# First image by image rows, first tile in float32, and MLP weights rebuilt from integer words: a pooled-attention + MLP kernel

## Chip, core and metric

The kernel runs on one core of a Trainium2 chip. The metric is the device time of one launch in microseconds (us), the median of several runs; lower is better. The engines are named as in the profile: PE (TensorE; PEld is its weight load), DVE (VectorE), ACT (ScalarE), POOL (GpSimd) and SP (SyncE, which issues the DMAs). Each engine works through its own instructions in order and waits where an operand or a buffer is not ready.

## What is computed

```python
# q (4, 12288, 128), kv (4, 384, 32, 128), w_sr (128, 128): float32
kv_pool = kv.reshape(B, H // 4, 4, W // 4, 4, C).mean(axis=(2, 4))
k = v = kv_pool.reshape(B, -1, C) @ w_sr             # 768 keys per image
s = (q @ k.transpose(0, 2, 1)) / np.sqrt(C)
a = np.exp(s - s.max(-1, keepdims=True))
a /= a.sum(-1, keepdims=True) + 1e-09
x = (a @ v).reshape(49152, 128)
h = x @ w_in                                         # w_in (128, 2048): float64
g = 0.5 * h * (1.0 + erf(h / np.sqrt(2.0)))
out = g @ w_out                                      # w_out (2048, 128): float64
```

The two weight matrices arrive as float64. [...]

## The kernel before

The 49152 tokens go in 96 tiles of 512 (24 tiles per image). A tile passes: queries scaled and split into a float16 high and low part, turned by a DMA transpose (`q_max`, `q_scale`, `q_split`, `q_turn`); scores of 128 tokens at a time against the 768 keys, as three float16 products (`score`, L365); evacuation with the running minimum (`evac`, L378); `exp`; division and split into float16 parts (`attn_hi`, `attn_lo`); a DMA transpose (`attn_turn`); the product with the values (`av`, 18 matmuls of 512 columns); `x_out`; then for each of 16 blocks of the MLP `mlp_in` (three matmuls), `gelu`, a float16 split (`rest`) and `mlp_out` (three matmuls).

All instructions stand in an order written by hand. The table `START` (L22) holds the order up to the first block of tile 1; behind it a loop (L737) runs tiles 1 to 95, in which each `mlp_in` of a tile stands beside the `mlp_out` six blocks back (`LAG`), beside the scores of the tile two ahead and the `av` of the next one. "Loop start" below is the first `mlp_in` of tile 1, the first row behind `START` on PE.

In `START` the first image is loaded in 24 DMAs of 256 KB (`kv_load_first`, L174), in which a partition receives 2 KB runs (four pixels of one row). DVE adds the 16 pixels of a pool window (`kv_sum_part`, L184), PE turns the sum, ACT scales it, PE multiplies by `w_sr` (`kv_key`) into `kT`, the keys in float32. Only when the largest key of the image is known (`kv_max`, `kv_bound`) can the keys be split in float16 (`kv_high`, `kv_low`) and the scores of tile 0 begin.

The weights are built in eight pieces of 512 columns (`w_split`, L649): ACT makes the absolute value of the upper word and a scaled lower word; DVE shifts and masks the words to a float32; ACT or DVE scales and casts to the float16 high part; POOL makes the low part with three float32 operations (L681 to L683). `w_max` and `w_scale` find the scale first. All eight pieces stand inside `START`, between the blocks of tile 0.

PSUM: `ps_h` has three buffers for blocks and half scores, `ps_s` one for the scores of 128 tokens, so the next `score` waits for the `evac` of the last.

Of the kernel before, what the change touches and what calls it, by code (L numbers as in the profile page):

```python
# [9 lines left out]
F32 = mybir.dt.float32  # L10
# [12 lines left out]
    ("q_load", 0), ("kv_load", 0), ("kv_load", 1), ("w_sr",), ("kv_load", 2),  # L23
    ("q_max", 0), ("q_scale", 0), ("q_split", 0), ("kv_load", 3), ("kv_load", 4), ("kv_load", 5),
    ("q_load", 1), ("kv_load", 6), ("q_turn", 0), ("kv_load", 7), ("kv_load", 8), ("kv_load", 9),
    ("kv_load", 10), ("kv_load", 11), ("wi_load", 0), ("wi_load", 1), ("wi_load", 2),
    ("wi_load", 3), ("q_load", 2), ("wo_load", 0), ("wo_load", 1),
    ("kv_sum", 0, 0), ("kv_sum", 0, 1), ("kv_sum", 1, 0), ("kv_turn", 0), ("kv_key", 0),
    ("kv_sum", 1, 1), ("kv_sum", 2, 0), ("kv_sum", 2, 1), ("kv_turn", 1), ("kv_key", 1),
    ("q_max", 1), ("q_scale", 1), ("q_split", 1), ("kv_turn", 2), ("kv_sum", 3, 0),  # L30
    ("kv_sum", 3, 1), ("kv_key", 2), ("kv_max", 0), ("kv_sum", 4, 0), ("kv_turn", 3),
    ("kv_key", 3), ("kv_sum", 4, 1), ("q_turn", 1), ("kv_sum", 5, 0), ("kv_sum", 5, 1),
    ("kv_turn", 4), ("kv_key", 4), ("kv_turn", 5), ("kv_key", 5), ("kv_max", 1), ("kv_bound", 0),
    ("w_split", 0, 0), ("kv_bound", 1), ("w_max", 0), ("kv_bound", 2), ("kv_high", 0),
# [791 lines left out]
```

## Time and profile before

| | |
|---|---|
| runs (us) | 2857.69, 2857.76, 2859.03; median 2857.76 |
| span of the profiled execution | 2856.5 us, first to last instruction |
| the profiled execution's own time | not listed apart from the runs; the median stands 1.26 us over its span |
| busy: PE, DVE, ACT, POOL | 2771.2, 2427.1, 2527.1, 891.6 us |
| in the stretch 165 to 2800 us | PE 2633.29 of 2635.00 us busy |

A row of the timeline gives the start, the time taken, engine, line, operation, what is written and read, and in brackets how long the engine sat idle before it and what released it. A row of the windows gives a stretch, then the busy time and number of instructions of each engine, the granted clock of PE, the DMA share and GB/s. A row of the groups gives busy time and mean duration.

### The profile page before, as it was taken

The numbers are of one execution on the slowest core, as the hardware profiler recorded it, in microseconds if no ns is written. First come the engines' busy times: TensorE is split into PE (matmuls) and PEld (weight loads), VectorE is DVE, ScalarE is ACT, GpSimd is POOL, SyncE is SP. The second block draws the span as 40 slices with busy tenths as digits, with TensorE's granted clock in tenths as the row PEclk, the third lists the DMA queues.
The fourth block names the chain that finished last, engine by engine and source line by source line (L and its number), as shares of the span: only waits on it lengthen the run. The fifth ranks groups of instructions, "written<-read, shape, count | busy, mean of one in ns | idle before, by whom it ended". The sixth has DMA issues, their size and how long they took to land.

```text
span 2856.5 us, 37679 instructions
## 1 busy us (share of the span) xinstructions
PE 2771.2 (97%) x13390; PEld 1316.0 (46%) x13390; DVE 2427.1 (85%) x3565; ACT 2527.1 (88%) x3414; POOL 891.6 (31%) x825
## 2 busy tenths in 40 slices
PE   3699999999999999999999999999999999999999
PEld 2244444444444444444444444444444444444444
DVE  7988888898888888889888888888888888888885
ACT  2589999999999999999999999999999999999997
POOL 2544343222233434222223343413222222222221
PEclk9799999999999999999999999999999999999999
DMA  7165555445445555445445655544544444444442
GB/s 198 35 124 109 105 108 107 91 94 98 93 106 109 105 124 106 95 91 100 91 95 102 124 105 107 106 95 87 104 92 94 92 94 93 94 92 94 90 93 49
DMA packets 854717, 284.90 MB, mean 100 GB/s; under 512 B 814848, under 2 KB 817280, under 8 KB 854528
## 3 DMA queue, kind: packets, MB, share of 16 engines
q1 hardware_dynamic: 854528, 282.49, 48.6%
q8 instruction: 105, 1.72, 0.2%
q14 instruction: 84, 0.69, 0.1%
HBM read 54.59 MB, written 25.17 MB: 28 GB/s over the span
## 4 chain that ended last, share of the span: by engine, by line
PE 91%; DVE 4%; DMA 2%; ACT 1%; issue 1%; POOL 1%; SPq 0%; DVEq 0%; POOLq 0%; ACTq 0%
PE s L372 12%; PE px L492 12%; PE po L542 11%; PE po L543 11%; PE po L544 11%; PE h L513 11%; PE h L512 11%; PE h L511 11%; DMA kv<-in_kv_dram 1%; DVE gl L531 1%; DVE a L454 1%; DMA q_v<-q_u 0%; DVE a L450 0%; DMA q<-in_q_dram 0%; DVE sn L383 0%
## 5 line engine op out<-in xcount | busy, mean ns | idle before, releaser
L525 ACT ACTIVATE g<-h,hs 128x512 f32<-128x512 f32 x1536 | 1007.1, 681 | 236.7 <-PE h L513 198.5
L531 DVE SCALAR_TENSOR_TENSOR gl<-g,gs,gh 128x1024 f16<-128x1024 f32 x768 | 1017.1, 1337 | 27.0 <-ACT gh L527 18.5
L527 ACT ACTIVATE gh<-g,gs 128x1024 f16<-128x1024 f32 x768 | 881.9, 1148 | 25.2
L544 PE MATMUL po<-gh,wo_l 128*128 128x512 f16 x1536 | 583.4, 380 | 13.6 <-POOL wo_l L683 13.6
L542 PE MATMUL po<-gh,wo_h 128*128 128x512 f16 x1536 | 582.9, 380 | 4.7 <-DVE wo_h L678 2.9
L511 PE MATMUL h<-xh,wi_h 128*128 128x512 f16 x1536 | 583.9, 380 | 1.2 <-DVE sn L419 0.6
L512 PE MATMUL h<-xl,wi_h 128*128 128x512 f16 x1536 | 583.5, 380 | 0.4 <-DVE xl L503 0.4
L513 PE MATMUL h<-xh,wi_l 128*128 128x512 f16 x1536 | 583.2, 380 | 0.0
L543 PE MATMUL po<-gl,wo_h 128*128 128x512 f16 x1536 | 582.8, 379 | 0.2 <-DVE gl L531 0.2
L345 POOL TENSOR_TENSOR q<-q,qi 128x512 f32<-128x512 f32 x96 | 100.9, 1051 | 1481.6 <-DVE qi L337 1288.8
L383 DVE TENSOR_SCALAR_CACHE_REDUCE sn<-s,sg 128x768 f32<-128x768 f32 x378 | 382.7, 1013 | 71.1 <-PE s L372 67.8
L372 PE MATMUL s<-k,q_v 128*128 128x384 f16 x2268 | 434.3, 328 | 6.5 <-DVE sn L383 5.1
L454 DVE SCALAR_TENSOR_TENSOR a<-sn,r,a 128x768 f16<-128x768 f32 x384 | 413.0, 1076 | 15.1 <-ACT a L450 1.6
L492 PE MATMUL px<-aT,v 128*128 128x512 f16 x1710 | 416.9, 380 | 2.0 <-DMA aT<-a 2.0
L430 ACT ACTIVATE sn<-sn,nm 128x768 f32<-128x768 f32 x384 | 354.6, 924 | 14.2 <-DVE nm L424 12.0
L372 PEld LDWEIGHTS <-q_v 128*128 128x128 f16 x2268 | 222.7, 98 | 197.1 <-issue 9.9
L443 DVE TENSOR_SCALAR r<-sum 128x2 f32<-128x2 f32 (+2 forms) x191 | 61.3, 321 | 241.6 <-ACT sn L430 241.6
L492 PEld LDWEIGHTS <-v 128*128 128x128 f16 x1710 | 167.5, 98 | 204.7 <-DMA aT<-a 2.5
L450 DVE TENSOR_SCALAR a<-sn,r 128x768 f16<-128x768 f32 x381 | 253.3, 665 | 7.1 <-DVE r L446 0.5
L319 POOL COPY o<-o_v 128x512 uint16<-128x512 uint16 x190 | 151.8, 842 | 323.4 <-DMA o_v<-o_u 318.6
L544 PEld LDWEIGHTS <-wo_l 128*128 128x128 f16 x1536 | 150.4, 98 | 197.0 <-POOL wo_l L683 15.1
L513 PEld LDWEIGHTS <-wi_l 128*128 128x128 f16 x1536 | 150.7, 98 | 183.0 <-issue 1.9
(118 smaller groups left out, 2163.4 us busy)
## 6 DMA issues: line engine op xcount, KB each, us to landing
q<-in_q_dram SPq DMA_DIRECT2D x96, 256.0 KB, 3.2
kv<-in_kv_dram SPq DMA_DIRECT2D x96, 256.0 KB, 4.8
out_dram<-o SPq DMA_DIRECT2D x95, 256.0 KB, 2.0
aT<-a SPq DMA_TRANSPOSE x384, 3.7
wi<-in_moe_w_in_dram SPq DMA_DIRECT2D x4, 512.0 KB, 9.7
wo<-in_moe_w_out_dram SPq DMA_DIRECT2D x4, 512.0 KB, 7.8
q_v<-q_u SPq DMA_TRANSPOSE x96, 3.1
o_v<-o_u SPq DMA_TRANSPOSE x95, 3.2
```

Source lines behind the costliest of these rows:

```text
L372: nc.tensor.matmul(ps[:, n, :KH], lhs[:, c], rhs[:, n * KH : (n + 1) * KH], start=rhs is kh and lhs is qh, stop=lhs is ql,)
L454: nc.vector.scalar_tensor_tensor(a[:, 1, :], st.pop(("s", t, c)), st["r", t][:, c : c + 1], a[:, 0, :], op0=ALU.mult, op1=ALU.subtract,)
L492: nc.tensor.matmul(ps, v[:, w, :], aT[:, :, o + k, :], start=k == 0 and i == 0, stop=k == KB - 1 and i == 2,)
L511: nc.tensor.matmul(ps, wi_h[:, fs], xh, start=True, stop=False)
L512: nc.tensor.matmul(ps, wi_h[:, fs], xl, start=False, stop=False)
L513: nc.tensor.matmul(ps, wi_l[:, fs], xh, start=False, stop=True)
L525: nc.scalar.activation(g[:, e, :], ps, AF.Gelu, scale=st["hs", b])
L527: nc.scalar.mul(gh, g, st["gs", b])
L531: nc.vector.scalar_tensor_tensor(gl, st["g", t, p], st["gs", t // TPB], st["gh", t, p], op0=ALU.mult, op1=ALU.subtract)
L542: nc.tensor.matmul(ps, wo_h[:, f, :], gh[:, e, :], start=f == 0, stop=False)
L543: nc.tensor.matmul(ps, wo_h[:, f, :], gl[:, e, :], start=False, stop=False)
L544: nc.tensor.matmul(ps, wo_l[:, f, :], gh[:, e, :], start=False, stop=f == FB - 1)
```

## The change

Everything happens in `START` and the functions that it calls; the loop is the same code.

- **Loads.** The first image comes in six DMAs of 1 MB (`kv_in`; the last in two parts): a partition receives half an image row, one run of 8 KB. w_in and w_out come behind it in four pieces of 1024 columns; the pool `stage` has six buffers instead of two.
- **Pooling.** DVE adds pixel pairs along the row (`kv_add`, 1024 and 512 elements); the sum over four rows, the turning and the factor 1/16 are one float32 product with a 128x32 matrix (`kv_pool`).
- **Tile 0 in float32.** Queries turned on PE (`q_turn_first`); scores, attention x values and both MLP products each one float32 matmul in place of three float16 ones; the attention is turned by PE transposes and copies in place of split and DMA; no `rest`. The scores start on the first half of the keys and do not wait for `kv_bound`.
- **Weights.** Each piece is first made a float32 array `wa` by one multiplication on ACT and three integer operations on DVE (`w_single`); tile 0 uses `wa` itself. From `wa` the float16 parts for tile 1 and later are made later, with one ACT and one DVE operation (`w_half`). POOL has no part in it.
- Queries of tiles 1 and 2 are split by ACT and DVE (`q_halves`) instead of POOL.

The core of the diff (`...` marks what is left out):

```diff
-    stage = ctx.enter_context(tc.tile_pool(name="stage", bufs=2))
+    stage = ctx.enter_context(tc.tile_pool(name="stage", bufs=6))
...
+    rows = kv[0].rearrange("(g p) w c -> g p (w c)", p=P)
+    def kv_in(h, n=0, parts=1):
...
+        nc.sync.dma_start(
+            st["row", h][:, n * w : (n + 1) * w],
+            rows[h // 2][:, (h % 2) * 2048 + n * w : (h % 2) * 2048 + (n + 1) * w],
+        )
+    def kv_add(h, n=0, parts=1):
+        v = st["row", h].rearrange("p (j w c) -> p j w c", w=R, c=C)
+        v = v[:, n * 4 // parts : (n + 1) * 4 // parts]
+        nc.vector.tensor_tensor(v[:, :, :2], v[:, :, :2], v[:, :, 2:], op=ALU.add)
+        nc.vector.tensor_tensor(v[:, :, 0], v[:, :, 0], v[:, :, 1], op=ALU.add)
+    def kv_pool(h):
...
+        for j in range(4):
+            nc.tensor.matmul(
+                ps[:, j * P // 4 : (j + 1) * P // 4], v[:, j, 0], pool32, start=True, stop=True
+            )
...
+        nc.scalar.copy(st["pT"][:, h], ps[:, :P])
+    def q_halves(t, step):
...
+            if step == 0:
+                nc.scalar.mul(u[:, 0, c], x[:, c], i[:, c : c + 1])
+            else:
+                nc.vector.scalar_tensor_tensor(
+                    u[:, 1, c], x[:, c], i[:, c : c + 1], u[:, 0, c],
+                    op0=ALU.mult, op1=ALU.subtract,
+                )
+    def attn_turn_first(c, n):
...
+        for k in range(3):
+            nc.tensor.transpose(
+                ps[:, k * P : (k + 1) * P],
+                st["s", 0, c][:, (3 * n + k) * P : (3 * n + k + 1) * P], ident,
+            )
...
-        for i, (lhs, rhs) in enumerate(((qh, kh), (ql, kh), (qh, kl))):
-            nc.tensor.matmul(ps, lhs[:, c], rhs[:, ks], start=i == 0, stop=i == 2)
+        if t == 0:
+            nc.tensor.matmul(ps, st["q32"][:, c], st["kT", 0][:, ks], start=True, stop=True)
...
+    def av_pair(n):
...
+            nc.tensor.matmul(
+                st["x", 0, n][:, : T // 2], st["v32"][:, k], st["aT", 0][:, k, ns],
+                start=k == 0, stop=k == KB - 1,
+            )
...
     def mlp_in(t, f):
+        if t == 0:
+            nc.tensor.matmul(ps, wa[:, fs], st["x32"], start=True, stop=True)
...
     def mlp_out(t, f):
+        if t == 0:
+            nc.tensor.matmul(
+                ps, wa[:, DFF + f * C : DFF + (f + 1) * C], st["g", 0, f // 2][:, e, :],
+                start=f == 0, stop=f == FB - 1,
+            )
...
+    def w_single(j, step):
+        w = st["w", j].rearrange("p (n e) -> p n e", e=2)
+        up, low = w[:, :, 1], w[:, :, 0].bitcast(U32)
+        if step == 0:
+            st["wy", j] = gp.tile([P, WL], F32, tag="g", name=f"wy_{j}")
+            nc.scalar.mul(st["wy", j], up.bitcast(F32), DOWN)
+        if step == 1:
+            nc.vector.tensor_scalar(low, low, 29, None, op0=ALU.logical_shift_right)
+        if step == 2:
+            nc.vector.scalar_tensor_tensor(
+                up, up, -0x80000000, w[:, :, 0], op0=ALU.bitwise_and, op1=ALU.bitwise_or
+            )
+        if step == 3:
+            nc.vector.scalar_tensor_tensor(
+                wa[:, j * WL : (j + 1) * WL].bitcast(I32), st.pop(("wy", j)).bitcast(I32), 3, up,
+                op0=ALU.logical_shift_left, op1=ALU.bitwise_or,
+            )
...
-            nc.gpsimd.tensor_tensor(l, l, a, op=ALU.mult)
-            nc.gpsimd.tensor_tensor(v, v, hi, op=ALU.subtract)
-            nc.gpsimd.tensor_tensor(lo, v, l, op=ALU.add)
+    def w_half(j, step):
+        a, inv = wa[:, j * WL : (j + 1) * WL], st["inv", j // NW]
...
+            nc.scalar.mul(hi[:, ws], a, inv)
...
+                lo[:, ws], a, inv, hi[:, ws], op0=ALU.mult, op1=ALU.subtract
...
-    ("w_split", 7, 3), ("x_out", 1), ("mlp_in", 0, 14), ("gelu", 0, 14), ("mlp_out", 0, 9),
     ("recips", 2, 0, 4), ("attn_hi", 2, 0, "dve"), ("attn_lo", 2, 0), ("attn_turn", 2, 0),
-    ("mlp_in", 0, 15), ("gelu", 0, 15), ("score", 3, 0), ("evac", 3, 0),
+    ("score", 3, 0), ("evac", 3, 0), ("w_half", 2, 1), ("w_half", 3, 1), 
```

How the order moves is seen best on the engines. On PE, before, these rows stand between the last key product and the scores of tile 0 (`pk` the key product, `km_ps` the search for the largest key, `s` the scores, `q_v` the turned queries):

```order
L212 MATMUL pk_5_313<-pT_5_311,w_sr_sb 128x128
L233 MATMUL km_ps<-km_d,ones 128x128
L407 LDWEIGHTS q_v
L407 MATMUL s_0_0_347<-k_337,q_v 128x384
L407 LDWEIGHTS q_v
L407 MATMUL s_0_0_347<-k_337,q_v 128x384
L407 LDWEIGHTS q_v
L407 MATMUL s_0_0_347<-k_337,q_v 128x384
```

In the change the same place on PE reads (`pp` the pooling product, `pv` the values in float32, `pa` the turned attention):

```order
L511 MATMUL s_2_0_238<-kT_182,q_171 128x384
L511 MATMUL s_3_0_240<-kT_182,q_171 128x384
L231 MATMUL pk_242<-pT,w_sr_sb 128x128
L206 MATMUL pp_252<-pool_126,row_150 128x32 x4
L231 MATMUL pk_258<-pT,w_sr_sb 128x128
L511 MATMUL s_0_0_210<-kT_182,q_171 128x384
L511 MATMUL s_1_1_289<-kT_182,q_171 128x384
L511 MATMUL s_2_1_291<-kT_182,q_171 128x384
L511 MATMUL s_3_1_296<-kT_182,q_171 128x384
L220 MATMUL pv_302<-w_sr_sb,pT 128x128 x3
L454 MATMUL pa_0_315<-ident,sn_0_227 128x128 x3
```

Half of the scores now stand among the pooling products, and the search for the largest key stands behind the first transposes of the attention.

On DVE, before, one weight piece inside the stretch of tile 0's blocks (`wt` the work tile, `gl` the low part of tile 0's blocks, `a_1` the attention of tile 1):

```order
L531 SCALAR_TENSOR_TENSOR gl_1_698<-g_2_667,gs_464,gh_2_668 128x1024
L664 TENSOR_SCALAR wt_700<-wi_189 128x512
L667 SCALAR_TENSOR_TENSOR wt_700<-wi_189,wt_700 128x512
L670 SCALAR_TENSOR_TENSOR wt_700<-wt_700 128x512
L677 TENSOR_SCALAR wt_700<-wt_700,inv_445 128x512
L678 CAST wi_h<-wt_700 128x512
L680 TENSOR_SCALAR wt_700<-wt_700 128x512
```

In the change, in the same stretch (`sn` the evacuated scores of tile 1):

```order
L727 SCALAR_TENSOR_TENSOR wa<-wy_385,w_158 128x1024
L489 TENSOR_SCALAR sn_0_440,nm_438<-s_0_431,sg_417 128x768
L721 TENSOR_SCALAR w_160<-w_160 128x1024
L723 SCALAR_TENSOR_TENSOR w_160<-w_160 128x1024
L489 TENSOR_SCALAR sn_1_458,nm_438<-s_1_451,sg_417 128x768
L727 SCALAR_TENSOR_TENSOR wa<-wy_429,w_160 128x1024
```

Three operations on 1024 columns stand where six on 512 stood, and the rows of `gl` are gone from the stretch.

The end of `START` on DVE in the change (`qi` the scale of tile 3's queries, `omega` that of w_out, `a_0` the attention of tile 2, `s_0_726` the first scores of tile 3):

```order
L387 TENSOR_SCALAR qi_698<-qe_697 128x4
L429 TENSOR_SCALAR sg_708<-qe_697,ks_355 128x4
L288 TENSOR_REDUCE omega_m<-omega_ps 128x1
L774 COPY omega<-omega_m 128x1
L775 RECIPROCAL inv_712<-omega_m 128x1
L341 TENSOR_SCALAR os_547<-hs_545,omega 128x1
L553 TENSOR_SCALAR r_718<-sum_604 128x4
L557 RECIPROCAL r_718<-r_718 128x4
L561 TENSOR_SCALAR a_0_721<-sn_0_605,r_718 128x768
L565 SCALAR_TENSOR_TENSOR a_0_721<-sn_0_605,r_718,a_0_721 128x768
L489 TENSOR_SCALAR sn_0_735,nm_733<-s_0_726,sg_708 128x768
```

Nine rows lie between the scale of tile 3's queries and the evacuation of their first scores; before, 22 rows lay between them.

More of the change, by code (lines that the diff above doesn't have):

```diff
@@ L22 @@
 START = [
[L23 to L34, printed above, removed]
@@ new lines @@
+    ("mlp_out", 0, 0), ("score", 1, 3), ("evac", 1, 3), ("mlp_out", 0, 1), ("mlp_in", 0, 6), ("gelu", 0, 6),
+    ("mlp_in", 0, 7), ("gelu", 0, 7), ("w_max", 1), ("w_scale", 0, 0), ("q_halves", 2, 1), ("q_turn", 2), ("q_sigma", 2), ("q_load", 3),
+    ("mlp_out", 0, 2), ("mlp_out", 0, 3), ("mlp_out", 0, 4), ("w_scale", 0, 1), ("w_scale", 0, 2), ("mlp_scale",),
+    ("exp", 1, 0), ("exp", 1, 1), ("w_half", 0, 0),
+    ("recips", 1, 0, 2), ("attn_hi", 1, 0, "dve"), ("attn_lo", 1, 0), ("attn_turn", 1, 0), ("exp", 1, 2), ("exp", 1, 3), ("attn_hi", 1, 1, "dve"), ("attn_lo", 1, 1), ("attn_turn", 1, 1), ("w_half", 0, 1),
@@ new lines @@
+    ("mlp_out", 0, 5), ("mlp_in", 0, 8), ("gelu", 0, 8), ("recips", 1, 2, 2), ("attn_hi", 1, 2, "act"),
+    ("mlp_in", 0, 9), ("gelu", 0, 9), ("attn_hi", 1, 3, "act"),
+    ("w_single", 3, 1), ("attn_lo", 1, 2), ("attn_turn", 1, 2), ("attn_lo", 1, 3), ("attn_turn", 1, 3),
+    ("mlp_out", 0, 6), ("mlp_out", 0, 7), ("w_single", 3, 2), ("w_single", 3, 3),
+    ("mlp_in", 0, 10), ("gelu", 0, 10), ("score", 2, 0), ("evac", 2, 0), ("w_half", 1, 0),
+    ("mlp_in", 0, 11), ("gelu", 0, 11),
+    ("score", 2, 1), ("evac", 2, 1), ("w_half", 1, 1),
@@ new lines, in kv_nat, with kv_key_first @@
+    def kv_nat(n):
+        if n == 0:
+            st["v32"] = ap_.tile([P, KB, C], F32, tag="a", name="v32")
+        ps = ps_h.tile([P, T], F32, tag="ps_h", name=f"pv_{n}")
+        for k in range(3):
+            nc.tensor.matmul(
+                ps[:, k * C : (k + 1) * C], st["pT"][:, 3 * n + k], w_sr_sb, start=True, stop=True
+            )
+        nc.scalar.copy(
+            st["v32"][:, 3 * n : 3 * n + 3].rearrange("p k c -> p (k c)"), ps[:, : 3 * C]
+        )
+    def kv_key_first(h):
+        if h == 0:
+            st["kT", 0] = prep.tile([P, KEYS], F32, tag="kT", name="kT_0")
+        ps = ps_h.tile([P, T], F32, tag="ps_h", name=f"pk_{h}")
+        nc.tensor.matmul(ps[:, :P], w_sr_sb, st["pT"][:, h], start=True, stop=True)
+        nc.scalar.copy(st["kT", 0][:, h * P : (h + 1) * P], ps[:, :P])
@@ L572, in o_join @@
         nc.sync.dma_start(out_t[t], o)
[L575 to L590 removed]
+    wa = wap.tile([P, 2 * DFF], F32, name="wa")
@@ new lines, in pooled_attention_mlp, with w_load @@
+    wi_c = w_in.rearrange("p (j w) -> j p w", w=WL)
+    wo_c = w_out_p.rearrange("p (j f) c -> j p f c", f=WL // C)
+    NW = DFF // WL
+    def w_load(j, n=0, parts=1):
+        if n == 0:
+            st["w", j] = stage.tile([P, 2 * WL], I32, tag="stage", name=f"w_{j}")
+        t = st["w", j]
+        if j < NW:
+            w = WL // parts
+            nc.sync.dma_start(
+                t[:, 2 * n * w : 2 * (n + 1) * w], wi_c[j][:, n * w : (n + 1) * w].bitcast(I32)
+            )
+        else:
+            nc.sync.dma_start(
+                t.rearrange("p (f c) -> p f c", c=2 * C), wo_c[j - NW].bitcast(I32)
+            )
```

296 lines of the change are left out of this document (145 added, 151 removed).

## The prediction

> **What bounds the kernel now.** First the busy time by stretch: columns are the stretch, its length, then busy us (instructions) of PE, PEld, DVE, ACT, POOL, the granted clock, DMA share, GB/s.
>
> ```profile
> 0.00:35.66 35.66, 7.58 (x18) 4.08 (x18) 23.63 (x51) 4.62 (x14) 7.24 (x13) 1.00 1.00 255
> 35.66:68.93 33.27, 15.85 (x119) 10.17 (x119) 25.92 (x74) 13.24 (x22) 4.80 (x4) 0.79 0.62 151
> 68.93:136.97 68.04, 39.15 (x134) 15.69 (x134) 63.44 (x103) 36.17 (x55) 36.52 (x26) 0.77 0.16 31
> 136.97:165.00 28.03, 24.64 (x120) 11.37 (x118) 24.52 (x33) 23.30 (x31) 13.62 (x13) 1.00 0.61 132
> 165.00:2800.00 2635.00, 2633.29 (x12772) 1252.03 (x12771) 2260.70 (x3279) 2406.69 (x3240) 820.68 (x764) 1.00 0.49 100
> ```
>
> From 165 us on PE is never idle: that part is the same code and stays. All the change can move lies ahead. Three rows mark the stages: the last key is written (35.66), tile 0's first block starts on PE (68.93), tile 1's first block, the loop start (136.97).
>
> ```profile
> 35.38 0.28 ACT L213 ACTIVATE kT<-pk 128x128 f32<-128x128 f32 x1 [0.88 <-PE pk L212]
> 68.93 0.38 PE L511 MATMUL h<-xh,wi_h 128*128 128x512 f16 x1 [0.60 <-DVE xh L502]
> 136.97 0.38 PE L511 MATMUL h<-xh,wi_h 128*128 128x512 f16 x1
> ```
>
> Stage 1 is loads (DMA share 1.00); stages 2 and 3 are DVE: 25.92 of 33.27 and 63.44 of 68.04. The waits of PE up to 165 us say the same (total, times, longest): DVE's scales and the weight pieces that DVE and POOL make.
>
> ```profile
> PE rho_ps L233 <- DVE rho_d L227: 13.8, 1, 13.8
> PE po L544 <- POOL wo_l L683: 13.6, 3, 5.4
> PE omega_ps L233 <- DVE omega_d L227: 5.3, 1, 5.3
> PE po L542 <- DVE wo_h L678: 2.9, 2, 1.5
> ```
>
> So the sum is: how early the loop starts, plus what changes in its first 28 us.
>
> **Stage 1, to the last key: 31 us (before 35.66).** Rate of the DMAs in 40 slices of the first 45 us, then DVE's two kinds of addition:
>
> ```profile
> GB/s 0 49 262 290 275 288 250 265 282 270 277 275 275 220 228 249 154 293 233 233 233 228 235 231 233 233 233 288 408 411 393 408 355 351 350 241 122 144 205 0
> 8.63 0.68 DVE L187 TENSOR_TENSOR u<-kv 128x512 f32<-128x512 f32 x1
> 9.35 0.42 DVE L188 TENSOR_TENSOR u<-u 128x256 f32<-128x256 f32 x1
> ```
>
> The image (2 KB runs) came at 220 to 290 GB/s; behind it the weights (4 KB runs, partitions 16 KB apart) at 350 to 411. The new loads have 8 KB runs, also 16 KB apart; I take 375, the weights' mean, with 233 as the other end. 6.29 MB then take 16.8 us (27.0). With 3.5 us for queries and w_sr ahead and about 1 us to land, the last half image is there at 21.3 (31.5), the first at 7.3. DVE: from the rows 1.03 ns per element more, so 1024 elements cost 1.22 and the 512 behind them 0.68; 1.9 per half, 11.4 in all instead of 18.4 for the sums, no bound. PE becomes one, because each half needs four float32 products with a new stationary operand:
>
> ```profile
> 11.38 0.50 PEld L212 LDWEIGHTS pk<-pT,w_sr_sb 128*128 128x128 f32 x2 [0.66 <-ACT pT L205]
> 11.38 0.79 PE L212 MATMUL pk<-pT,w_sr_sb 128*128 128x128 f32 x2 [0.37 <-ACT pT L205]
> 218.01 0.41 PEld L212 LDWEIGHTS pk<-pT,w_sr_sb 128*128 128x128 f32 x2
> 218.22 0.39 PE L212 MATMUL pk<-pT,w_sr_sb 128*128 128x128 f32 x2
> 218.44 0.38 PE L542 MATMUL po<-gh,wo_h 128*128 128x512 f16 x1
> ```
>
> A float32 product is two passes (x2), each with its own load: 0.20 us a load in the steady stretch, 0.25 early. Four products: 1.6 to 2.0; copy to `pT` and its waits 0.6; key product 0.4 to 0.8. Six halves at 2.6 to 3.4 from 9.2 (first half plus DVE) give 25 to 30, the four half scores among them 2.6 to 5.1, the last copy 0.3: 28 to 35. I take 31, nearer the full clock, because PE is now busy three parts in four. Held to 233 GB/s it is 31.5 + 1 + 3.5 = 36.
>
> [...]
>
> **Stage 2, last key to tile 0's first block: 24 us (before 33.27).** Gone from the path: the search for the largest key and the split (4 us, 35.66 to the first score at 39.5), half of the scores, all `attn_lo`, the DMA transposes, and the wait for w_in's scale, 13.8 us above. New price of a float32 matmul: the two passes of 128 columns at 218.22 end where the next matmul starts, 0.22 later; four columns' worth of float16 time, so 512 columns cost 0.86 where three float16 matmuls cost 0.65 (0.22 each: the 14 loads of 384 columns at 42.31, quoted below, stand 0.167 apart). Rows used here and in stage 3:
>
> ```profile
> 39.47 5.58 PE L407 MATMUL s<-k,q_v 128*128 128x384 f16 x24 [1.79 <-ACT k L267]
> 47.81 0.62 DVE L450 TENSOR_SCALAR a<-sn,r 128x768 f16<-128x768 f32 x1
> 48.47 1.02 DVE L454 SCALAR_TENSOR_TENSOR a<-sn,r,a 128x768 f16<-128x768 f32 x1
> 58.71 0.42 DVE L664 TENSOR_SCALAR wt<-wi 128x512 int32<-128x512 int32 x1
> 59.16 0.69 DVE L667 SCALAR_TENSOR_TENSOR wt<-wi,wt 128x512 int32<-128x512 int32 x1
> 63.44 1.34 POOL L682 TENSOR_TENSOR wt<-wt,wi_h 128x512 f32<-128x512 f32 x1
> 63.80 1.53 DVE L667 SCALAR_TENSOR_TENSOR wt<-wi,wt 128x512 int32<-128x512 int32 x1
> 82.28 1.28 DVE L531 SCALAR_TENSOR_TENSOR gl<-g,gs,gh 128x1024 f16<-128x1024 f32 x1
> L419 DVE TENSOR_SCALAR_CACHE_REDUCE sn<-s,sg 128x384 f32<-128x384 f32 x12 | 6.9, 612 | 2.7 <-PE s L407 2.7
> L383 DVE TENSOR_SCALAR_CACHE_REDUCE sn<-s,sg 128x768 f32<-128x768 f32 x6 | 6.1, 1013 | 0.3
> ```
>
> DVE's work: four half evacuations 2.5; four divisions at 0.62, 2.5; four copies of 384 from PSUM at 0.61, as an evacuation, 2.4; maximum, bound and key split 3.4; two word operations at 1.23 (0.69 for 512, plus 512 elements at 1.03 ns) 2.5; some fifteen small ones and the last copy 2.6. Sum 15.9. On top 8 us in which DVE waits for PE: 1.0 for the first score; 2.7 while the first pair of attention x values (six matmuls of 256, 0.43 each) stands ahead of the third transposes; 2 for the second pair; 2.3 for transposes and the bound's product. PE itself needs about 15. Bounds: 20 if most waits close, 30 at half clock (PE 15 becomes 25 to 30).
>
> **Stage 3, tile 0's first block to loop start: 55 us (before 68.04).** DVE's list: six word operations at 1.23 (7.4) and three shifts at 0.7 (2.1); four maxima over 1024 as those (4.9); two low parts as L531 (2.6); nine evacuations at 1.01 (9.1); three `attn_hi` (1.9), five `attn_lo` (5.1); query maxima and low parts (2.6); `x_out` (1.5); 36 small ones at 0.19 (6.8). Sum 44.0 instead of 63.44: seven `gl` rows and half the weight work are gone, and POOL is quiet, whose activity is what made the same L667 take 1.53 (POOL was in L682 then) and 0.69 (POOL idle). Word operations in place on every second word are not in the trace: 0.42 and 1.53 x 2 are the ends, 1.23 the nearest row scaled.
>
> Waits in stage 3: 2.3 because `wy` and the `g` pairs share three buffers, so ACT's gelu of block 4 waits for two `mlp_out` and the exponentials behind it come late; 1.0 for `attn_hi` on ACT; 1.2 for the third half-tile score, since `ps_s` has one buffer; 3 for tile 1's `av`. Then the end. `score` 3,0 stands on PE ahead of the loop start and needs tile 3's queries, scaled late on DVE (about 40 us of its 44), split on POOL, turned by DMA:
>
> ```profile
> 4.83 1.04 POOL L345 TENSOR_TENSOR q<-q,qi 128x512 f32<-128x512 f32 x1 [3.42 <-DVE qi L337]
> 5.94 0.61 POOL L346 CAST q_u<-q 128x512 f16<-128x512 f32 x1
> 6.63 1.48 POOL L347 TENSOR_TENSOR q_u<-q,q_u 128x512 f16<-128x512 f32 x1
> q_v<-q_u SPq DMA_TRANSPOSE x96, 3.1
> ```
>
> 3.2 + 3.1 + 1.0 for the scores = 7.3. So 40 + 7.5 + 7.3 = 55. PE's own work is 26 float32 matmuls (22.4) and 13 us of float16, 35 in all: covered as long as the clock is full. Bounds: 48 if the waits close, 62 if the word operations cost half as much again.
>
> **Loop and sum.** Six `mlp_out` of tile 0 fall in the loop at 0.86 instead of 0.65: +1.3. These waits stand in the first stretch of the loop before:
>
> ```profile
> 152.76 1.14 PE L372 MATMUL s<-k,q_v 128*128 128x384 f16 x6 [1.37 <-DVE sn L383]
> 157.21 1.47 PE L492 MATMUL px<-aT,v 128*128 128x512 f16 x6 [2.02 <-DMA aT<-a]
> ```
>
> 3.4 us, as DVE was behind; DVE now starts with 2.6 us of `w_half` but with no `gl` of tile 0, so I keep 1: -2.4. Loop start 31 + 24 + 55 = 110, 27 earlier than 136.97. Span 2856.5 - 27 - 1.1 = 2828.4; the runs' median, 2857.76, stands 1.26 over the span, so **2830**. All shorter ends together (28, 20, 48) would give 2816, all longer (36, 30, 62) 2848.
>
> **Rivals.**
> *Loads no faster.* The image stays at 233 GB/s, or the pooling products at half clock: stage 1 is 36 to 37. For it: DMA share is 1.00 already. Against: the 408. 2836 to 2846 with a slower stage 2. 0.15.
> *Waits close.* 2 and 3 run near DVE's sums (20, 48): 2816 to 2821. For it: DVE was busy 93% of stage 3. Against: float32 chains on PE have fewer rows beside them. 0.15.
> *The clock: slower than before.* PE is granted half clock in sparse stretches. The loads' spacing shows it (each ahead of a 384-column matmul):
>
> ```profile
> 41.99 0.15 PEld L407 LDWEIGHTS <-q_v 128*128 128x128 f16 x1 [0.17 <-issue]
> 42.31 2.34 PEld L407 LDWEIGHTS <-q_v 128*128 128x128 f16 x14 [0.17 <-issue]
> ```
>
> 0.32 apart, then 0.17, some 3 us after that burst began at 39.5. At half clock all through, stage 3's PE work is 70 instead of 35 and with waits 75; stage 2 is 30, stage 1 36; loop start 141, six cold blocks +4: 2864. It decides from a mean clock of about 0.55 in stage 3; the rows above have 0.77 with PE busy 39 of 68, and PE will be busier. 0.06, of which a third within 0.2%.
> *The change doesn't do what it says.* The word operations keep POOL's price without POOL: +11 in stage 3, 2841. 0.03.
>
> [...]
>
> **Chances.** Forecast (2822 to 2838) 0.61; the rivals as given. The measurement tells 0.2% (5.7 us) from no change: faster 0.94, within 0.02, slower 0.04. The range 2816 to 2846 leaves out the slow clock, the far ends of the two fast-and-slow rivals, under 0.2 together.
>
> **What would show it.** Right: last `kT` near 31, image at over 350 GB/s; first float32 block near 55 with no wait for `rho_d`; L723 and L727 at 1.2; loop start near 110, behind a wait of `score` 3,0 for `q_v`; float32 blocks 0.86 apart. Wrong: blocks 1.7 apart, DVE waiting for PE over 20 us in stage 3, or idle of PE past 165.

## The result, and the profile after

The change runs in 2821.52 us (median of 4 runs, 2820.46 to 2825.23), the kernel before, beside it, in 2857.73: ratio 0.9874, 95% interval 0.9860 to 0.9888. The prediction was 2830 with a range of 2816 to 2846; the stretch in which it put most of its chances, 2822 to 2838, begins just above the measured time. The profiled execution of the change has a span of 2819.5 us, 37.0 less than before.

| | before | predicted | after |
|---|---|---|---|
| stage 1, start to last key | 35.66 | 31 | 28.20 |
| stage 2, to tile 0's first block | 33.27 | 24 | 17.49 |
| stage 3, to the loop start | 68.04 | 55 | 56.03 |
| loop start | 136.97 | 110 | 101.72 |
| loop and end | 2719.53 | 1.1 less | 2717.78 |

The windows of the change, one row for each stage and one for the loop (columns as in the prediction: stretch, length, busy us of PE, PEld, DVE, ACT, POOL, granted clock, DMA share, GB/s). The 1.00 in the clock column of stage 1 is not to be taken at its word; the section on two kinds of executions says why.

```profile
0.00:28.20 28.20, 16.86 (x72) 13.66 (x72) 15.68 (x28) 5.06 (x15) 1.33 (x10) 1.00 0.94 362
28.20:45.69 17.49, 13.65 (x70) 10.22 (x70) 14.88 (x47) 12.02 (x24) 0.00 (x0) 1.00 0.46 103
45.69:101.72 56.03, 38.93 (x128) 18.05 (x129) 40.92 (x83) 31.06 (x48) 2.80 (x3) 0.87 0.22 50
165.00:2780.00 2615.00, 2612.78 (x12672) 1242.51 (x12671) 2220.99 (x3247) 2389.83 (x3219) 813.87 (x757) 1.00 0.43 100
```

DVE has lost 8 us in stage 1, 11 in stage 2 and 22.5 in stage 3; POOL, 36.5 us busy in the old stage 3, now has three rows there. Behind 165 us PE is full as before. The timeline has the stage marks and the wait that ends last ahead of the loop:

```profile
27.93 0.27 ACT L232 COPY kT<-pk 128x128 f32<-128x128 f32 x1 [0.58 <-PE pk L231]
45.69 1.98 PE L619 MATMUL h<-x,wa 128*128 128x512 f32 x4 [0.52 <-DVE ks L311]
99.83 2.10 PE L478 MATMUL s<-k,q_v 128*128 128x384 f16 x6 [6.46 <-DMA q_v<-q_u]
101.72 0.63 PE L622 MATMUL h<-xh,wi_h 128*128 128x512 f16 x1
```

The 13.8 us wait for `rho_d` in front of the first block has become 0.52 for `ks`, and the last wait of stage 3 is the one forecast, tile 3's scores for their turned queries. The waits of PE up to 165 us (total, times, longest) name one that the prediction did not have, the first row (it had 1.2 us for one such wait, for scores of tile 1):

```profile
PE s L478 <- DVE sn L489: 6.8, 2, 6.0
PE s L478 <- DMA q_v<-q_u: 6.5, 1, 6.5
PE h L619 <- ACT g L635: 2.1, 1, 2.1
PE omega_ps L283 <- DVE omega_d L277: 1.8, 1, 1.8
```

The rate of the loads in 40 slices of the change's first 45 us:

```profile
GB/s 0 95 273 251 408 401 430 408 444 430 415 437 437 404 379 295 368 424 421 455 408 401 370 354 346 349 350 330 115 131 0 7 0 0 0 0 0 2 210 138
```

The image comes at 400 to 440 for most of the stretch, where it came at 220 to 290 before.

### The profile page after: what moved, and what is told of

It is laid out like the page before. It is cut to its first block, busy times and chain, and to the rows that moved or that the text cites. A ratio compares the mean times of both kernels' runs of the same rounds, so it can differ in the third digit from the quotient of the medians.

```text
span 2819.5 us, 37507 instructions
## 1 busy us (share of the span) xinstructions
PE 2780.0 (99%) x13384; PEld 1329.3 (47%) x13384; DVE 2366.3 (84%) x3494; ACT 2518.4 (89%) x3411; POOL 847.0 (30%) x795
## 4 chain that ended last, share of the span: by engine, by line
PE 95%; DVE 2%; ACT 1%; DMA 1%; POOL 1%; issue 1%; SPq 0%; DVEq 0%; ACTq 0%; POOLq 0%
PE s L478 13%; PE px L600 12%; PE po L661 11%; PE po L660 11%; PE po L662 11%; PE h L622 11%; PE h L624 11%; PE h L623 11%; DVE a L565 0%; PE po L654 0%; DMA q_v<-q_u 0%; DVE gl L643 0%; PE pp L206 0%; ACT sn L540 0%; DVE a L561 0%
## 5 line engine op out<-in xcount | busy, mean ns | idle before, releaser
L635 ACT ACTIVATE g<-h,hs 128x512 f32<-128x512 f32 x1520 | 995.3, 680 | 213.4 <-PE h L624 169.8
L643 DVE SCALAR_TENSOR_TENSOR gl<-g,gs,gh 128x1024 f16<-128x1024 f32 x760 | 1004.2, 1334 | 27.0 <-ACT gh L637 18.1
L637 ACT ACTIVATE gh<-g,gs 128x1024 f16<-128x1024 f32 x760 | 872.7, 1148 | 24.8
L660 PE MATMUL po<-gh,wo_h 128*128 128x512 f16 x1520 | 576.1, 379 | 1.7 <-ACT oT L667 1.7
L661 PE MATMUL po<-gl,wo_h 128*128 128x512 f16 x1520 | 576.1, 379 | 0.4 <-DVE gl L643 0.4
L624 PE MATMUL h<-xh,wi_l 128*128 128x512 f16 x1520 | 576.3, 379 | 0.0
L623 PE MATMUL h<-xl,wi_h 128*128 128x512 f16 x1520 | 576.3, 379 | 0.0
L622 PE MATMUL h<-xh,wi_h 128*128 128x512 f16 x1520 | 576.3, 379 | 0.0
L662 PE MATMUL po<-gh,wo_l 128*128 128x512 f16 x1520 | 576.1, 379 | 0.0
L553 DVE TENSOR_SCALAR r<-sum 128x2 f32<-128x2 f32 (+1 forms) x193 | 40.8, 211 | 252.6 <-ACT sn L540 252.6
```

The costliest lines, as they stand in the source:

```text
L622: nc.tensor.matmul(ps, wi_h[:, fs], xh, start=True, stop=False)
L623: nc.tensor.matmul(ps, wi_h[:, fs], xl, start=False, stop=False)
L624: nc.tensor.matmul(ps, wi_l[:, fs], xh, start=False, stop=True)
L635: nc.scalar.activation(g[:, e, :], ps, AF.Gelu, scale=st["hs", b] if t > 0 else 1.0)
L637: nc.scalar.mul(st["gh", t, f // 2], g, st["gs", b])
L643: nc.vector.scalar_tensor_tensor(gl, st["g", t, p], st["gs", t // TPB], st["gh", t, p], op0=ALU.mult, op1=ALU.subtract)
```

## The experiments

The theory after the result: the three stages are three separate gains, each with one cause. Stage 1 is the loads, stage 2 the scores that need no scale, stage 3 the weights built without POOL.

### One part alone

The weights alone, in the kernel before (`w_split`, its eight pieces kept; the kernel reads each float64 weight as an upper and a lower 32-bit word):

```diff
-            nc.vector.tensor_scalar(
-                ai, up, 3, 0x3FFFFFFF, op0=ALU.logical_shift_left, op1=ALU.bitwise_and
...
+            nc.vector.tensor_scalar(low, low, 29, None, op0=ALU.logical_shift_right)
...
-            nc.gpsimd.tensor_tensor(l, l, a, op=ALU.mult)
-            nc.gpsimd.tensor_tensor(v, v, hi, op=ALU.subtract)
-            nc.gpsimd.tensor_tensor(lo, v, l, op=ALU.add)
+            nc.vector.scalar_tensor_tensor(lo, a, inv, hi, op0=ALU.mult, op1=ALU.subtract)
```

> The kernel before with one part of the change: the weights are rebuilt from integer words in the old eight pieces of 512 columns, without GpSimd; the scaled high part by ACT or DVE, the low part by one operation on DVE. Loads, float16 tile 0 and all else as before. Theory (the old price of stage 3 was the weight build on DVE and GpSimd): the waits of PE for wo_l and wo_h (13.6 and 2.9 us) go and the time falls by 12 to 20 us (ratio 0.993 to 0.996). Rival (tile 0's float16 splits were the price): the time falls by less than 5 us.

2845.93 us against 2858.14, ratio 0.9957 (0.9941 to 0.9974). Its stage 3:

```profile
68.20:124.55 56.35, 34.77 (x135) 14.83 (x134) 49.52 (x94) 33.31 (x47) 6.51 (x6) 0.82 0.20 38
```

56.35 us, against 68.04 before and 56.03 in the full change; the loop starts 12.4 earlier, as much as the span is shorter. So the weights alone bring as much as stage 3 gained in the change, with tile 0 still in float16 splits. The rival falls; that the float32 blocks of tile 0 also drop the rows of `gl` does not show in the length of this stage. The reverse, tile 0 in float32 with the old weights, was not run.

The loads and the pooling alone, in the kernel before (`kv_in`, `kv_add`, `kv_pool`, the key product without a scale, six image buffers):

```diff
-    ("kv_sum", 0, 0), ("kv_sum", 0, 1), ("kv_sum", 1, 0), ("kv_turn", 0), ("kv_key", 0),
+    ("kv_add", 0), ("kv_pool", 0), ("kv_key", 0), ("kv_add", 1), ("kv_pool", 1), ("kv_key", 1),
```

> The kernel before with the other end of the change: the first image in loads with 8 KB runs, DVE adding pixel pairs, and the 128x32 product on PE; scores, weights and tile 0 as before. Theory (the three stages add): the last key comes 7 to 8 us earlier, the loop start as much, and the time falls by 6 to 8 us. Rival (w_in's scale, the 13.8 us wait, sets the end of stage 2 whenever the keys come): the last key is 7 us earlier, but the loop start and the time move by less than 3 us.

2846.18 us, ratio 0.9958 (0.9943 to 0.9972). The last key is written at 28.10, 7.6 earlier, the first block starts at 62.29, 6.6 earlier, the loop at 130.96, 6.0 earlier: what stage 1 gains comes through two later stages almost whole, also through the wait for `rho_d`, which stays 13.6 us long and begins earlier. The rival falls. The span is 10.9 shorter, 4.9 more than the loop start, which nothing expected. PE's idle time in the loop accounts for most of it: 2719.53 less 2708.67 busy is 10.9 before, 2714.64 less 2707.54 is 7.1 here.

The two parts give 12.2 and 12.0 of the change's 36.2. But 4.9 of the second lie in the loop, where the change itself gained only 1.75, so the loop start is the better measure: the parts move it by 12.4 and 6.0 of 35.25. The other 16.8 us are left to tile 0 in float32, and 15.8 of them stand in stage 2. There the wait for `rho_d` stays 13.8 and 13.6 us long with either part alone, and in the change it is gone. So stage 2's cause is found by subtraction and from the order of the rows; tile 0 in float32 was not run alone.

### Does POOL's work slow DVE?

Six operations on POOL behind each weight piece, which nothing waits for, in the change:

```diff
+    def pool_back(j):
+        for n in range(2):
+            x = wa[:, j * WL + n * 512 : j * WL + (n + 1) * 512]
+            for op1 in (ALU.mult, ALU.subtract, ALU.add):
+                nc.gpsimd.tensor_tensor(scratch, x, x, op=op1)
```

> The changed kernel with 24 added operations of 128x512 float32 on GpSimd, six behind each of the four weight pieces, as many as the kernel before ran there; they read the finished weights and write a scratch tile that nothing reads, so nothing waits for them except through contention. Theory (GpSimd's activity had slowed DVE): DVE's rows of 1024 elements beside them go from 1.22 to 1.5 us or more, DVE's busy time between the first block and the loop start rises by 8 to 12 us, and the loop starts 5 to 10 us later than 101.7. Rival (only the waits for its results cost): DVE's rows stay at 1.22 and the loop start moves by less than 1.5 us.

Groups of DVE in stage 3 (count | busy us, mean ns | idle before), first of the change, then with POOL at work:

```profile
L723 DVE SCALAR_TENSOR_TENSOR w<-w 128x1024 int32<-128x1024 int32 x3 | 3.7, 1224 | 0.2
L727 DVE SCALAR_TENSOR_TENSOR wa<-wy,w 128x1024 int32<-128x1024 int32 x3 | 3.7, 1221 | 0.1
L411 DVE SCALAR_TENSOR_TENSOR q_u<-q,qi,q_u 128x128 f16<-128x128 f32 x4 | 1.1, 344 | 0.0
L721 DVE TENSOR_SCALAR w<-w 128x1024 uint32<-128x1024 uint32 x3 | 2.0, 682 | 0.0
```

```profile
49.69:109.99 60.30, 39.44 (x129) 17.66 (x129) 48.17 (x83) 31.00 (x48) 31.85 (x26) 0.88 0.20 46
L724 DVE SCALAR_TENSOR_TENSOR w<-w 128x1024 int32<-128x1024 int32 x3 | 5.0, 1654 | 0.2
L728 DVE SCALAR_TENSOR_TENSOR wa<-wy,w 128x1024 int32<-128x1024 int32 x3 | 4.4, 1461 | 0.1
L411 DVE SCALAR_TENSOR_TENSOR q_u<-q,qi,q_u 128x128 f16<-128x128 f32 x4 | 3.6, 962 | 0.0
L722 DVE TENSOR_SCALAR w<-w 128x1024 uint32<-128x1024 uint32 x3 | 2.0, 680 | 0.0
```

The same 83 operations on DVE take 48.17 us instead of 40.92, with 29 us of POOL beside them, and stage 3 is 4.3 us longer (60.30 against 56.03). The timeline shows that not every row suffers while POOL is busy (here from 48.34 to 72.89 us):

```profile
50.44 0.68 DVE L722 TENSOR_SCALAR w<-w 128x1024 uint32<-128x1024 uint32 x1
51.23 1.87 DVE L724 SCALAR_TENSOR_TENSOR w<-w 128x1024 int32<-128x1024 int32 x1
59.46 1.22 DVE L728 SCALAR_TENSOR_TENSOR wa<-wy,w 128x1024 int32<-128x1024 int32 x1
```

The shift, with one array, keeps its 0.68; of the four word operations on two arrays that fall into this time, three take 1.87 to 1.95 for 1.22. The theory holds for the rows; it was put slightly too high in DVE's time (8 to 12 expected, 7.25 measured). The loop starts 8.3 later, as expected (5 to 10), but half of that is something else: the last key, ahead of any added operation, came 4.0 late. That is taken up below. Nor need all of the 4.3 us of stage 3 be POOL's. In two kernels without its work whose last key came as late, stage 3 took 57.27 us (16 products of constants ahead, below) and 58.07 (runs of 2 KB, below), so that POOL adds between 2.2 and 4.3. As far as this measures what POOL cost before, it is the smaller part of the 12 us that the new weights are worth there. The rest goes with the shorter list (DVE 63.44 us busy before, 49.52 with the weights alone) and with PE's waits for `wo_l` and `wo_h`, 13.6 and 2.9 us, which are no longer among its waits; these two were not run apart.

### Why the loads became faster

The prediction set the length of a partition's run beside each rate. First the change with runs of 2 KB, in the same places:

```diff
+            for o in range(n * w, (n + 1) * w, 512):
+                nc.sync.dma_start(
+                    st["row", h][:, o : o + 512],
+                    rows[h // 2][:, (h % 2) * 2048 + o : (h % 2) * 2048 + o + 512],
+                )
```

> The changed kernel, its image loads cut into pieces of 256 KB in which a partition receives one run of 2 KB (8 KB before); everything behind them is the same. Theory (the run length sets the rate): the image comes at 233 to 290 GB/s as in the kernel before, the last key is written at 33 to 34 us instead of 28.2, and the time is 4 to 6 us over that of the change (2825.5 to 2827.5). [...]

Then the same 2 KB runs from the places of the kernel before:

```diff
+        for a in range(n * R // parts, (n + 1) * R // parts):
+            nc.sync.dma_start(st["row", h][:, a * W_C : (a + 1) * W_C], kv_h[0, h, a])
```

> The changed kernel with the first image fetched in the pieces of the kernel before: 256 KB each, one row of each pool window (a partition gets four pixels, 2 KB; eight partitions next to one another read 16 KB in a row, the next eight stand four image rows on). The pooling then adds other pixels than the reference does, so the keys are other sums; everything else is the same. Runs of 2 KB in the image-row layout came at 385 to 420 GB/s, so the length of the run is not the cause. Theory (the places read at one time set the rate): the image comes at 230 to 290 GB/s again, the last half lands at 29 to 32 us, and the time is 4 to 8 us above the change. Rival (the old rate came from the destination or from the many small issues): about 400 GB/s, last half before 25.5 us.

The window from 12 to 15 us (the last number is GB/s), first of the change, then of the 2 KB runs in the new places, then in the old places:

```profile
12.00:15.00 3.00, 2.41 (x11) 2.28 (x11) 2.31 (x3) 0.71 (x3) 0.00 (x0) 1.00 1.01 429
```

```profile
12.00:15.00 3.00, 2.65 (x13) 2.51 (x13) 2.16 (x3) 0.53 (x2) 0.00 (x0) 1.00 1.06 397
```

```profile
12.00:15.00 3.00, 2.25 (x10) 1.82 (x9) 1.92 (x2) 0.53 (x2) 0.00 (x0) 1.00 1.07 298
```

429, 397 and 298 GB/s. A quarter of the run length costs under a tenth; the old places cost another quarter, at the same run length and into the same tiles. The mean of the three windows from 9 to 18 us says the same: 405, 390 and 298. DVE begins on the fourth half image, for which it waits in all three kernels, at 15.39 in the change, 16.86 with short runs and 19.47 with the old places. So the run length is the smaller part, and the places that are read at one time are most of this difference: 2 or 8 KB from each of 128 image rows, 16 KB apart, against 16 rows, 64 KB apart, each read whole. The forecast for the old places was not met to the letter: 298 lies above its 230 to 290, and far from its rival's 400. The kernel before had 229 to 277 between 6 and 18 us; what separates this from 298 stays open.

The old places give 2828.79 us in the median, 7.3 over the change; a part of it is what the next section shows, since the profiled run, of 2825.00, is only 3.8 over the change's. The 2 KB runs gave 2829.60, 2822.19, 2822.31 and 2830.68: two runs within 1 us of the change, two 8 us above it. Their median of 2825.95 falls into the range that the wrong theory expected, and so does the profiled last key at 32.98. Neither comes from the loads.

### Two kinds of executions: when PE's clock comes up

In the profile of the 2 KB runs DVE begins on the half images 0.9 to 1.5 us later than in the change, and yet the last key is 4.8 us later. The timeline of PE shows the pooling products, first in the change:

```profile
12.82 1.76 PE L206 MATMUL pp<-pool,row 128*128 128x32 f32 x8
18.79 2.92 PE L511 MATMUL s<-kT,q 128*128 128x384 f32 x4 [0.35 <-ACT kT L232]
21.50 1.48 PE L206 MATMUL pp<-pool,row 128*128 128x32 f32 x8
23.66 0.98 PE L206 MATMUL pp<-pool,row 128*128 128x32 f32 x8
28.25 2.85 PE L511 MATMUL s<-kT,q 128*128 128x384 f32 x8 [0.36 <-ACT kT L232]
```

and with the 2 KB runs:

```profile
25.07 1.75 PE L207 MATMUL pp<-pool,row 128*128 128x32 f32 x8
29.77 1.75 PE L207 MATMUL pp<-pool,row 128*128 128x32 f32 x8
33.03 5.38 PE L512 MATMUL s<-kT,q 128*128 128x384 f32 x8 [0.35 <-ACT kT L233]
```

The same eight passes take 1.76 us, then 1.48 from 21.5 on, and 0.98 from 23.66 on; in the second kernel they are at 1.75 to the end, and the eight half-score passes still take 5.38 in place of 2.85. PE works at half speed until some moment, and that moment lies behind the first scores in one execution and behind the last key in the other. The clock column reads 1.00 over this stretch in both profiles; that half speed is half clock rests on the profile with products of constants, below, where the column goes from 0.98 to 0.50 and the same passes from 1.05 to 1.75. The kernel itself was therefore run again:

> The changed kernel itself, once more. The kernel with 2 KB runs and the one with GpSimd operations began, row for row, like the change, and yet their last key came at 32.7 and 31.9 us instead of 28.2, with pooling products of 1.75 us per half where the change's profile has 0.98 from 21.5 us on. Theory (PE's clock comes up in stage 1 in some executions and later in others): the runs spread over 5 to 9 us, in two or more groups, 2820 to 2822 and 2825 to 2830. Rival (the added operations or the 2 KB runs caused it): all runs within 2820 to 2823.

2820.77, 2821.53, 2821.60 and 2830.55; spans 2819.1 to 2819.9, and 2828.8. With the first four runs, two of eight are late, by 4 and 9 us. The kernel is the same, so the rival falls: nothing in the code decides between them. That PE's clock does is likely, not shown: the two late runs list a mean granted clock of 0.996 and the other six 0.997, but neither was profiled. Then PE was kept busy from 1.5 us on with products of constants:

```diff
+    ("warm", 4), ("q_turn_first",), ("warm", 12),
...
+            nc.tensor.matmul(ps[:, :P], ident, ones, start=True, stop=True)
```

> The changed kernel with 16 products of constants (128x128 float32) on PE ahead of the first pooling product, from about 2 to 9.6 us, into a PSUM bank that nothing reads. Theory (the clock): pooling runs at full clock from the first half on (0.98 instead of 1.75 us per half), the last key stands at 27 to 28 us in every execution, bound by the loads and DVE; the runs lie within 3 us of one another near 2820, as the luckiest of the change. Rival (the clock is not held by so sparse a stretch, or the variation has another cause): spread and median as the change.

Spans 2826.3, 2826.1, 2817.3 and 2817.9: still two groups, the short ones some 2 us below those of the change. The windows of a late one show the clock (third number from the right) go, and two rows of its pooling products what they cost on either side:

```profile
8.00:14.00 6.00, 3.16 (x23) 2.58 (x21) 4.47 (x5) 0.53 (x2) 0.00 (x0) 0.98 1.01 425
14.00:32.10 18.10, 15.84 (x51) 12.11 (x50) 11.52 (x24) 2.64 (x11) 0.00 (x0) 0.50 1.01 377
10.45 1.05 PE L206 MATMUL pp<-pool,row 128*128 128x32 f32 x8 [1.94 <-DVE row L198]
21.51 1.75 PE L206 MATMUL pp<-pool,row 128*128 128x32 f32 x8
```

It was full at the first pooling product, with PE busy 3.16 us of 6 it fell, and stayed at half for 18 us. With four more products of constants in the gaps of each of the first four halves:

```diff
-    ("kv_add", 0), ("kv_pool", 0), ("kv_key", 0), ...
+    ("kv_add", 0), ("kv_pool", 0), ("warm", 2), ("kv_key", 0), ("warm", 2), ...
```

> The changed kernel with the 16 products of constants ahead of the first half image, as before, and four more behind each of the first four pooling and key products, so that PE has no gap of more than half a microsecond from 1.5 us to the first scores. With the 16 alone the clock was up at 10 us and fell to 0.50 at about 14 us, among the pooling products of two halves, in two of four runs (2826.3 against 2817.3 us of span). Theory (the granted clock follows how full PE is, and the pooling stretch is too sparse for it): the clock stays at 1.00 to the scores in every run, the last key comes at 25.5 to 27.5 us, all spans lie at 2816 to 2818.5. Rival (a clock that comes up so early drops anyway, or 32-column products do not count): spans in two groups as with the 16 alone, the late ones even 1 to 3 us later because the added products run at half clock in front of the pooling.

```profile
8.00:25.31 17.31, 14.47 (x101) 12.51 (x100) 15.02 (x27) 3.19 (x12) 0.00 (x0) 1.00 1.01 403
25.04 0.27 ACT L232 COPY kT<-pk 128x128 f32<-128x128 f32 x1 [0.58 <-PE pk L231]
43.62 1.99 PE L625 MATMUL h<-x,wa 128*128 128x512 f32 x4 [0.52 <-DVE ks L311]
100.94 0.63 PE L628 MATMUL h<-xh,wi_h 128*128 128x512 f16 x1
```

In the profiled execution the clock holds, and the last key stands at 25.31, 2.9 earlier than in the change. The spans are 2817.7, 2818.2, 2820.6 and 2820.9: none 8 us late, but two groups all the same, and not within the 2816 to 2818.5 expected. Of the 2.9 us only 0.8 are left at the loop start: stage 2 is 0.8 us longer and stage 3 1.3, and its two 6 us waits stay. So the clock holds where it was profiled, as the theory had it, and its worth in the median is nothing (2821.13 against 2821.56). Whether the filling takes away the late runs, four runs do not show; the last kernel below, filled in the same way, lost the clock once more.

What decides when the clock comes up is not shown: behind a burst of 2.92 us of scores the pooling products were at full speed in one execution (the change, 0.98 from 23.66 on) and not in another (the 2 KB runs, 1.75 at 25.07).

### What sets stage 2

```diff
-    ("kv_low", 0), ("a_evac", 2, 0, "act"), ("w_single", 1, 0),
+    ("a_evac", 2, 0, "act"), ("w_single", 1, 0),
...
-    ... ("x_first", 0, "act"), ("kv_low", 1), ("kv_val",),
+    ... ("x_first", 0, "act"),
...
+    ... ("x_first", 1, "dve"), ("kv_low", 0), ("kv_low", 1), ("kv_val",),
```

> The changed kernel with three steps of stage 2 moved behind the last copy of tile 0's attention output: the two low halves of the keys on DVE (0.61 us each, 0.55 net) and the DMA turn of the values. Nothing ahead of the first block of the MLP needs them. Theory (stage 2 is DVE's list, its waits for PE are small): the first block starts 0.7 to 1.2 us sooner after the last key than the 17.5 us of the change, at the same clock; the rows come back behind it and the total gains less than 1 us. Rival (PE's chain of transposes and products sets stage 2, as the 8 us of waits in the prediction had it): 17.5 us stay, and DVE's two waits of 0.84 and 0.96 us grow by what was moved.

The last key stands at 27.65, the first block at 45.23: 17.58 us, as in the change (17.49), at full clock in both (twelve passes of `px` take 2.86 us in either). DVE's waits for PE in the change, then with the rows moved:

```profile
40.44 0.56 DVE L461 COPY aT<-pa 128x384 f32<-128x384 f32 x1 [0.84 <-PE pa L454]
45.22 0.42 DVE L469 COPY x<-px 128x256 f32<-128x256 f32 x1 [0.96 <-PE px L586]
```

```profile
39.94 0.56 DVE L461 COPY aT<-pa 128x384 f32<-128x384 f32 x1 [1.37 <-PE pa L454]
44.76 0.42 DVE L469 COPY x<-px 128x256 f32<-128x256 f32 x1 [1.52 <-PE px L586]
```

0.84 and 0.96 have become 1.37 and 1.52, by 1.09 us in all, what was moved. The theory falls and the rival holds: the chain through PE sets stage 2, and rows of DVE that nobody needs yet stand inside its waits for nothing. The runs (2823.28 to 2827.83) are slower than most of the change's; in the profiled one the loop starts 1.5 us later, at 103.22, with a last key 0.5 earlier; the moved rows now stand in stage 3.

### What sets the end of stage 3

Tile 3's queries earlier:

```diff
+    ("q_max", 3), ("q_scale", 3), ("q_split", 3), ("q_turn", 3), ("q_sigma", 3), ("x_out", 1),
...
-    ... ("w_scale", 1, 1), ("q_max", 3), ("q_scale", 3), ("q_split", 3), ("q_turn", 3), ("q_sigma", 3),
+    ... ("w_scale", 1, 1),
```

> The changed kernel with tile 3's queries scaled, split, turned ahead of the output of tile 1's attention (x_out), some 7 us earlier, where DVE stands idle for 2.9 us. Theory (the end of stage 3 is the chain maximum, scale, split on GpSimd, DMA turn, scores): the wait of the scores of tile 3 for the turned queries, 6.5 us, goes; the loop starts 4 to 6.5 us earlier and the time falls by 3 to 6 us against the change. Rival (DVE's list sets it): the wait is replaced by one for the exponentials of tile 2, the attention or buffers, and the time falls by under 1.5 us.

2816.23, 2817.22, 2822.97 and 2823.33. The profile is of a run with the late clock, so stage 3 is compared with the one of the 2 KB kernel, late as well (52.20 to 110.27, 58.07 us): it takes 49.70 us, 8.4 less (6.3 less than in the change), and the wait for `q_v` is not in the list of waits any more. The short runs are some 4.5 us below those of the change (2820.46 to 2821.82), the late ones some 7 below the late ones of the 2 KB kernel. The theory holds. Behind the loop start stand new waits of PE: 1.7 us for ACT's gelu in two pieces and 1.7 for a turned attention, a part of what did not reach the end.

Then also the evacuation of tile 2's first scores, ahead of the last weight piece on DVE. The same edit puts one `mlp_out` of tile 0 (block 8) behind the `mlp_in` and `gelu` of block 12, which the lines below leave out and no run separates:

```diff
+    ("score", 2, 0), ("evac", 2, 0), ("w_single", 3, 1), ("attn_lo", 1, 2), ...
...
-    ("mlp_in", 0, 10), ("gelu", 0, 10), ("score", 2, 0), ("evac", 2, 0), ("w_half", 1, 0),
+    ("mlp_in", 0, 10), ("gelu", 0, 10), ("w_half", 1, 0),
```

> The kernel with the early queries of tile 3, and also tile 2's first scores and their evacuation ahead of the last weight piece and of two low parts of the attention on DVE, so that the second scores need not wait 6.0 us for the one PSUM buffer. Theory (that wait holds PE and all behind it in order): the 6.0 us go, the loop starts 3 to 5 us earlier and the time falls by 2 to 5 us against the kernel with the early queries alone (its short runs 2816.2 to 2817.2). Rival (DVE's list sets this stretch): the wait moves to the product with the last weight piece and to av, which stand behind the same DVE rows; the time changes by under 1 us.

```profile
78.12 1.14 PE L479 MATMUL s<-k,q_v 128*128 128x384 f16 x6 [0.18 <-DVE sn L490]
82.99 2.07 PE L655 MATMUL po<-g,wa 128*128 128x512 f32 x2 [2.87 <-DVE wa L728]
97.98 0.38 PE L623 MATMUL h<-xh,wi_h 128*128 128x512 f16 x1
```

The 6.0 us are 0.18 now, and 2.87 wait for the last weight piece (L728) in their place: part of the rival too. Stage 3 is 45.89 us, 3.8 less. The runs are 2812.47, 2813.95, 2815.36 and 2818.80.

### Together

> The filled PE of stage 1 together with the early queries of tile 3 and the early evacuation. Theory (three causes at three places add): last key at 25 us as with the fill, first block at 43 to 45, stage 3 at 45 to 48 us as with the early evacuation (45.9), so the loop starts at 89 to 92 and all runs lie at 2810 to 2814, 7 to 11 us under the change, within 4 us of one another. Rival (what comes earlier in stage 1 waits again in stage 3, as the fill alone left a loop start of 100.9 after a key 2.9 us earlier): the loop starts at 93 to 96 and the runs lie within 1 us of the short ones of the early evacuation (2812.5 to 2814).

2808.97 us in the median of 5 (2807.79 to 2812.98) against 2858.22: ratio 0.9826 (0.9812 to 0.9839), 12.5 us under the change. The profiled execution is its longest (span 2811.2): the clock was full up to the 2.33 us in which PE waits for the first half image and 0.50 behind them (the window from 11 to 13 us), and the last key came at 31.52. Stage 3 took 44.34 us (49.09 to 93.43). The other spans are 2806.1 to 2808.4. So the gains add, to rather more than expected in the median. The rival's time fails with it (four of five runs lie below 2812.5), but its loop start, 93 to 96, is what the one profile has; a short run was not profiled, and that its loop starts earlier is inferred from its span. The runs spread over 5.2 us instead of 4, and the clock is not held in every execution. The filling leaves that first gap open, 2.33 us here and 1.95 in the filled kernel above, whose clock stayed; that the longer gap is the cause was not tested.

## Why the prediction was right, and where its sizes were off

**The mechanism.** The forecast was that all gain lies ahead of the loop, in three stages, and that the loop start sets the end. It does: the loop start moved by 35.25 us, the span by 37.0. The loop and its end gained 1.75 (1.1 predicted).

**Stage 1, 31 against 28.20.** The price of DVE's additions (1.22 and 0.69) was as worked out, and so was that of PE's eight passes while they were slow (1.76, forecast 1.6 to 2.0); at full speed they took 0.98, below the lowest that it had. That PE becomes the bound was right: from the first pooling product on (9.99) it is busy 15.77 of 18.21 us, the scores that DVE waits for stand ahead of the fifth half image's additions, and with the clock held the key came at 25.31 from the same loads. The load rate was set at 375 and is 400 to 440. Longer runs, which the prediction set beside the higher rate, are not the reason in the main: runs of 2 KB came at about 390. The row of before that carried the argument, 233 for the image and 408 for the weights, had the length and the places changed at once. Changed one at a time, the length gave under a tenth (429 to 397 GB/s) and the places a quarter (397 to 298). The 1 us that the sum allows for a load to land was an estimate; DVE began on the first half image at 7.94 us, against the 7.3 of the sum.

**Stage 2, 24 against 17.49: the mis-sized term.** The step "on top 8 us in which DVE waits for PE" failed. DVE's list was put at 15.9 and measured 14.88; its idle time is 2.6 instead of 8. The waits were added to a list that also held the rows that stand inside them: the low halves of the keys, the word operations. Moving the low halves out left the stage as long as it was, and made the waits longer by just their time; the word operations were not moved. The list and the chain should have been two bounds, of which the longer counts, and not a sum. The half clock as the upper bound (30) did not come either:

```profile
36.89 2.86 PE L586 MATMUL px<-aT,v 128*128 128x256 f32 x12 [0.24 <-ACT aT L461]
39.58 1.60 PE L454 MATMUL pa<-ident,sn 128*128 128x128 f32 x12
```

Twelve passes of transposes take 1.60 us, 0.13 each, between products at full speed. So the transposes are as fast as the passes of the values beside them (`pv`, six of 128 columns in 0.83 us, 0.14 each).

**Stage 3, 55 against 56.03: right, with errors that cancel.** Up to the scale of tile 3's queries it took 48.28 us (47.5 predicted), of which DVE was busy 37.39 (40); the waits are 10.9 instead of 7.5, above all because PE stood 6.0 us for the evacuation of tile 2's first scores, which the list did not have. The end chain took 7.75 us (7.3). The cause of the gain is shown by the weights alone: with tile 0 in float16 the stage is as short.

**The rivals.** *Loads no faster* and *the word operations keep POOL's price* did not happen: 400 to 440 GB/s; 1.22 us for 1024 words. The other half of the first, pooling at half clock, came true in the late executions, with a last key at 32 to 33 instead of 36 to 37. *Waits close* came true for stage 2, which ended even below its 20, and not for stage 3; the time of 2821.52 lies next to its 2816 to 2821 by stage 2 (6.5 us under the forecast) and by stage 1 (2.8), of which it had said nothing. *The clock*: half speed is there in stage 1, for the first half images in each profile without products of constants, and the late runs of the change lost 4 and 9 us. Stage 3's mean clock is 0.87, far from the 0.55 at which it would have decided.

## What to carry to other kernels

When an engine's work and its waits for another engine are both known, do not add them: ask first which rows of its own list can stand inside those waits, and take the longer of the list and the chain. Before a rate is put down to one property of a transfer, look for what else differs between the fast and the slow row, and change that one thing alone. A time that spreads in two groups over runs of one kernel is first a question of which execution was profiled; compare stages between executions whose early part went alike.
